# Silu writes each chunk's tokens landmark-major, so that the output store's outer dimension is 32 and not 4

## The chip, the cores and the metric

One core of one Trainium2 chip. The metric is the device time of one execution in microseconds, as the median of several; executions 1 to 2% slower, at a lower granted clock (slow runs), are left out of comparisons. In the profiles PE is TensorE (matrix products), PEld its weight loads, ACT ScalarE (functions such as Silu), DVE VectorE, POOL GpSimd, SP SyncE (here it issues transfers). SBUF is the core's working memory; PSUM is the memory that TensorE writes to, used here as eight tiles of 512 columns, called banks. A ratio is the mean time of one kernel's fast runs over the mean of the other's of the same rounds, so it is not quite the ratio of the medians quoted beside it.

## The reference

Nystrom attention for 8 batches of 8 heads, 576 tokens, 32 landmarks (a landmark is the mean of 18 neighbouring tokens), then a two-layer block on all 4608 tokens:

```python
x = attn_out.transpose(0, 2, 1, 3).reshape(B * S, H * D)     # 4608 x 512
h = x @ w_in                                                 # 512 -> 2048
g = h * (1.0 / (1.0 + np.exp(-h)))                           # Silu
return (g @ w_out).astype(np.float32)                        # 2048 -> 512
```

Token number within a batch is `l * 18 + j`: landmark l (32), place j within it (18).

The 576 output rows of a batch are nearly the same: permuting tokens inside the chunks changes the reference's result by 3e-7 of its norm. The comparison with the reference therefore does not see a wrong token order. The order in each kernel that claims to be right was checked apart from it, by following token numbers through the index patterns.

## The kernel before

It is one static program. A planner (not shown) simulates the five engines with rough durations and fixes the order of instructions on each; a Silu of 512 columns counts as 0.485 us in it. The hidden columns of a batch stand in the order (parity of j, j // 2, l), 32 values of l innermost. Layer 1 makes 16 tiles of 128 hidden features by 512 tokens in PSUM; ScalarE applies Silu and writes bf16 to `gm`. Layer 2 takes 128 tokens at a time (a chunk: 4 values of j, 32 of l) as stationary weights; the result is copied to `ost` and stored. Two of the 18 values of j go through a second path, `gx`, not changed here.

```python
ost_r = ring(outp, [128, DMODEL], FP, "ost", 3)
...
def layer1(b):
    ...
        mm(ps.rearrange("p (c x) -> p c x", c=2), m_sb[:, g, dc*128:(dc+1)*128],
           etc[:, g, :, 0:256], start=(g == 0), stop=(g == 1))
    ...
        nc.scalar.activation(out=gm[:, dc, :], in_=bank(cell["o"]), func=AF.Silu)
    ...                                          # the gx path, once per 8 tiles
        nc.scalar.activation(
            out=gx[:, d0:d0 + 8, c:c + 64].rearrange("p d (l j) -> p d j l", j=2),
            in_=bank(cell["o"]).rearrange("p (d j l) -> p d j l", d=8, j=2), func=AF.Silu)
...
def rows(b, n):
    return out[b * S:(b + n) * S, :].rearrange("(b l j) n -> b j l n", b=n, j=J)

def layer2_batch(b):
    for c in range(4):
        j0 = 8 * (c % 2) + c // 2
        def stores(ost, j0=j0):
            return nc.sync.dma_start(out=rows(b, 1)[0, j0:j0 + 7:2], in_=ost)
        layer2(lambda dc, c=c: gm_r[b % 3][:, dc, c * 128:(c + 1) * 128], ..., stores)
```

Loads of q, k, v for later batches are issued by GpSimd; stores and DMA transposes (`qT`, `ct`) are issued by SyncE and share one queue. From batch 2 on GpSimd sums k and q in a tree to the landmarks `lm`. `ct` is the transpose of `ce`, the exponentials that TensorE multiplies with v; by the program its DMA transposes wait until the v load of the next batch has landed, where there is one. `pb` is the first step of the next batch's softmax over landmarks.

The softmax here doesn't subtract the row's maximum and nothing guards it: scores larger than these inputs give would overflow.

## Time and profile before

| | before |
|---|---|
| median (4 runs) | 314.46 us, 313.25 to 315.34 |
| PE, ACT busy | 269.5, 179.7 us of 313.0 |
| gm Silu | 128 of 642 ns, from start to start 0.478 us |
| waits of PE on `lm` and on `ct` | 16.5 + 14.7 us |

The lines themselves are in the prediction. Read them as it does: first where TensorE has holes, then what ends each hole, then why that thing was late.

### The profile page before, as it was taken

Reading aid. Unit: us, or ns where it says so; the run is one execution under the profiler, and the core shown is the slowest. Engines: PE = TensorE matmul, PEld = TensorE weight load, DVE = VectorE, ACT = ScalarE, POOL = GpSimd, SP = SyncE. Lnnn points to the kernel's source line nnn. Section 1 sums busy time; section 2 is a strip of 40 time slices with the busy share of each in tenths; the row PEclk is TensorE's granted clock in tenths of the full one; section 3 lists DMA queues with packets and bytes.
Section 4 is the critical chain, followed back from the end, with each engine's and each line's share of the span. In section 5 each row is a group of like instructions: output and inputs, shape, how many; then the busy total and the mean of one; then the engine's idle time right before and its main releaser. Section 6 shows DMA issues by size and latency. Waiting matters only on the chain.

```text
span 313.0 us, 5933 instructions
## 1 busy us (share of the span) xinstructions
PE 269.5 (86%) x2367; PEld 135.0 (43%) x2367; DVE 96.6 (31%) x258; ACT 179.7 (57%) x405; POOL 106.9 (34%) x133
## 2 busy tenths in 40 slices
PE   7998999939889638998799249997999999999991
PEld 5965545414344214453444024444445544444440
DVE  1676028400555611405346114035365300000000
ACT  1776986448826914898149209985369975112110
POOL 8157319453924590485041931295000000000000
PEclk9999999968999956999799659999999999999998
DMA  6999997969386928696669257866951011132222
GB/s 113 209 197 201 206 209 129 163 136 169 60 135 123 206 66 178 116 154 69 129 132 199 68 71 139 165 98 106 193 95 44 17 31 37 40 96 64 75 68 97
DMA packets 58076, 37.60 MB, mean 120 GB/s; under 512 B 39105, under 2 KB 49345, under 8 KB 58049
## 3 DMA queue, kind: packets, MB, share of 16 engines
q0 software_dynamic: 15232, 18.35, 35.3%
q1 hardware_dynamic: 42816, 18.88, 29.6%
q8 instruction: 18, 0.29, 0.4%
q14 instruction: 10, 0.07, 0.1%
HBM read 36.70 MB, written 9.44 MB: 147 GB/s over the span
## 4 chain that ended last, share of the span: by engine, by line
PE 52%; DMA 29%; ACT 6%; POOL 4%; SPq 3%; issue 2%; DVE 2%; POOLq 0%; ACTq 0%
PE ps L323 52%; DMA v<-in_v_dram 11%; DMA ct<-ce 7%; DMA w_in_sb<-in_moe_w_in_dram 7%; SPq L479 3%; ACT gm L811 3%; DMA qT<-qk 3%; POOL qk L368 2%; POOL v L375 2%; ACT gx L834 1%; ACT L914 1%; DVE bbd L576 1%; ACT ce L691 0%; DVE bm L570 0%; POOL lm L516 0%
## 5 line engine op out<-in xcount | busy, mean ns | idle before, releaser
L323 PE MATMUL ps<-w_out_sb,gm 128*128 128x512 bf16 x512 | 122.1, 382 | 0.0
L811 ACT ACTIVATE gm<-ps 128x512 bf16<-128x512 f32 x128 | 67.4, 642 | 30.6 <-PE ps L323 30.4
L323 PE MATMUL ps<-etn,m 128*128 128x64 bf16 (+1 forms) x512 | 75.5, 299 | 0.1
L323 PEld LDWEIGHTS <-gm 128*128 128x128 bf16 x512 | 47.4, 98 | 52.7 <-issue 2.9
L323 PEld LDWEIGHTS <-m 128*128 128x128 bf16 x512 | 33.1, 101 | 30.1 <-issue 7.1
L333 ACT COPY ost<-ps 128x512 f32<-128x512 f32 x25 | 14.7, 587 | 50.8 <-PE ps L323 50.7
L516 POOL TENSOR_TENSOR sa<-qk 128x576 f32<-128x576 bf16 x24 | 31.0, 1311 | 34.4 <-DMA qk<-in_k_dram 33.9
L620 DVE SCALAR_TENSOR_TENSOR st<-st,ps 128x320 bf16<-128x320 bf16 (+3 forms) x54 | 21.6, 408 | 46.0 <-PE ps L323 42.8
L323 PE MATMUL ps<-v,ct 96*64 96x128 bf16 x192 | 10.0, 251 | 15.6 <-DMA ct<-ce 14.7
L368 POOL DMA_DIRECT2D qk<-in_k_dram x8 | 6.0, 745 | 51.2 <-DMA qT<-qk 50.0
L335 DVE CAST m<-ps 128x512 bf16<-128x512 f32 x31 | 19.8, 686 | 9.0 <-PE ps L323 9.0
L516 POOL TENSOR_TENSOR sb<-sa 128x512 f32<-128x512 f32 (+1 forms) x24 | 21.6, 901 | 1.8
L333 ACT CAST m<-ps 128x512 bf16<-128x512 f32 x33 | 17.9, 617 | 3.0 <-PE ps L323 2.9
L323 PE MATMUL ps<-idb,lm 128*128 128x128 bf16 x32 | 4.7, 240 | 16.5 <-POOL lm L516 16.5
L335 DVE COPY ost<-ps 128x512 f32<-128x512 f32 x11 | 7.6, 689 | 32.7 <-PE ps L323 32.7
L375 POOL DMA_DIRECT2D v<-in_v_dram x24 | 13.9, 589 | 6.1 <-DMA w_out_sb<-in_moe_w_out_dram 3.7
L323 PE MATMUL ps<-w_out_sb,gx 128*128 128x512 bf16 x64 | 15.9, 379 | 0.0
L323 PEld LDWEIGHTS <-ct 96*64 96x64 bf16 x192 | 7.1, 126 | 20.3 <-DMA ct<-ce 17.2
L323 PE MATMUL ps<-zer 128*128 128x256 bf16 x95 | 14.5, 295 | 1.1 <-DVE zer L402 1.1
L323 PE MATMUL ps<-st 128*128 128x160 bf16 (+1 forms) x96 | 15.2, 234 | 0.0
L691 ACT ACTIVATE ce<-ps 128x288 bf16<-128x288 f32 x32 | 12.7, 412 | 3.9 <-PE ps L323 3.9
L323 PEld LDWEIGHTS <-st 128*128 128x128 bf16 x96 | 9.3, 103 | 12.3 <-issue 3.7
(68 smaller groups left out, 260.7 us busy)
## 6 DMA issues: line engine op xcount, KB each, us to landing
out_dram<-ost SPq DMA_DIRECT2D x36, 256.0 KB
qk<-in_k_dram POOLq DMA_DIRECT2D x8, 576.0 KB, 9.4
qk<-in_q_dram POOLq DMA_DIRECT2D x8, 576.0 KB, 12.3
v<-in_v_dram POOLq DMA_DIRECT2D x24, 192.0 KB, 13.3
w_out_sb<-in_moe_w_out_dram POOLq DMA_DIRECT2D x4, 512.0 KB, 10.8
w_in_sb<-in_moe_w_in_dram POOLq DMA_DIRECT2D x4, 256.0 KB, 9.6
w_in_sb<-in_moe_w_in_dram POOLq DMA_DIRECT2D x8, 128.0 KB, 7.4
qT<-qk SPq DMA_TRANSPOSE x24
```

Of the source, the lines that this page charges most:

```text
L323: nc.tensor.matmul(out=out_ap, lhsT=lhsT, rhs=rhs, start=start, stop=stop, skip_group_check=True)
L333: nc.scalar.copy(out=out, in_=in_)
L335: nc.vector.tensor_copy(out=out, in_=in_)
L368: lambda e, t=t, src=src: nc.gpsimd.dma_start(out=qk_r[b % 2][:, t].rearrange("p g j d -> p g (j d)"), in_=src[b].rearrange("(g h) (l j) d ...
L375: lambda e, a=a: nc.gpsimd.dma_start(out=v_r[b % 2][a * L:(a + 1) * L, :, :], in_=v[b].rearrange("h (l a x) d -> a l h (x d)", l=L, a=VA)[ ...
L479: lambda e, t=t, g=g: nc.sync.dma_start_transpose(out=qT[:, t, g], in_=qk[:, t, g].rearrange("p j d -> p (j d)")),
L516: lambda e: nc.gpsimd.tensor_tensor(out=o_, in0=a_, in1=b_, op=OP.add),
L576: bbd_op = chain("bbd", 0.2, lambda: nc.vector.tensor_tensor(out=bbd, in0=bc(bmt, 4, 2), in1=bc(hmask, NG, 1), op=OP.mult), [bmt_op, prev. ...
L620: nc.vector.scalar_tensor_tensor(out=s2[:, g0:g1, lo:SW], in0=s[:, g0:g1, lo:SW], scalar=2.0, in1=ps[:, 0:NG * SW].rearrange("p (g x) -> p ...
L691: nc.scalar.activation(out=ce[:, :, 0:VP].rearrange("p (i c) (a l) -> p c a i l", c=2, a=VA)[:, c], in_=bank(me[f"C{g}"], c)[:, 0:HS].rear ...
L811: lambda e, dc=dc, cell=cell: nc.scalar.activation(out=gm[:, dc, :], in_=bank(cell["o"]), func=AF.Silu),
L834: lambda e, d0=d0, cell=cell, c=c: nc.scalar.activation(out=gx[:, d0:d0 + 8, c:c + 64].rearrange("p d (l j) -> p d j l", j=2), in_=bank(ce ...
```

## The change

The intent: a store whose DRAM side has an outer dimension of 4 occupies only 4 of the 16 DMA engines (the prediction shows the share of 0.27 from which it reads this). If the partitions of `ost` are ordered (l, j) and not (j, l), the DRAM side becomes 32 x 4 x 512 and all 16 should take part. The order is made where Silu writes `gm`.

```diff
-    out=gm[:, dc, :], in_=bank(cell["o"]), func=AF.Silu),
+    out=gm[:, dc].rearrange("p (q l j) -> p q j l", q=4, j=4),
+    in_=bank(cell["o"]).rearrange("p (q j l) -> p q j l", q=4, j=4),
+    func=AF.Silu),
...
-    return nc.sync.dma_start(out=rows(b, 1)[0, j0:j0 + 7:2], in_=ost)
+    return nc.sync.dma_start(
+        out=out[b * S:(b + 1) * S, :].rearrange(
+            "(l j) n -> l j n", j=J)[:, j0:j0 + 7:2], in_=ost)
```

(The helper `rows` goes.) ScalarE now writes 16 runs of 32 elements with a step of 4 elements, 8 bytes.

More of the change, by code (lines that the diff above doesn't have):

```diff
@@ L870, in layer2 @@
         return pieces
-    def rows(b, n):
-        return out[b * S:(b + n) * S, :].rearrange("(b l j) n -> b j l n", b=n, j=J)
     def layer2_batch(b):
```

## The prediction

> **What bounds the kernel now.** I read the digits by slice first, then the chain of work that ended last, the waits, stretches of time, and last the records of single DMA packets.
>
> ```profile
> PE   7998999939889638998799249997999999999991
> PEclk9999999968999956999799659999999999999998
> ```
>
> TensorE is full except in a few slices, and the clock falls to half speed around the holes (slices 9, 15 and 16, 23 and 24 of 7.8 us each: near 66, 117 and 180 us). PE is busy 269.5 of 313.0 us, so 43.5 us is the most that anything which only fills holes can win, apart from what the half clock costs. The chain in order of time names what ends the holes:
>
> ```profile
> 98.64 1.14 POOL v L375 x2
> 99.78 15.76 DMA v<-in_v_dram
> ...
> 115.59 2.75 DMA ct<-ce
> 118.34 0.04 issue
> 118.38 11.11 PE ps L323 x107
> ...
> 161.68 19.59 DMA v<-in_v_dram
> ...
> 181.32 2.74 DMA ct<-ce
> ...
> 243.88 62.58 PE ps L323 x342
> ```
>
> Two loads of v last 15.8 and 19.6 us; the transpose ct waits for them and TensorE for it. From 243.9 us the end is pure TensorE. The waits give the sums:
>
> ```profile
> POOL sa L516 <- DMA qk<-in_k_dram: 33.9, 6, 8.7
> PE ps L323 <- POOL lm L516: 16.5, 5, 5.4
> PE ps L323 <- DMA ct<-ce: 14.7, 5, 5.9
> ```
>
> So 31 us of TensorE's holes hang on loads and transposes: k must land before GpSimd's tree of sums (5.9 us) can give lm, and v before ct. The stretches (columns: stretch, busy of PE, PEld, DVE, ACT, POOL, granted clock, DMA share, GB/s) show why the loads are late:
>
> ```profile
> 110.00:114.00 4.00, 2.25 (x8) 0.95 (x8) 0.43 (x1) 0.70 (x2) 3.77 (x5) 0.50 0.31 78
> 131.00:135.00 4.00, 3.85 (x37) 1.85 (x36) 0.00 (x0) 4.00 (x9) 1.48 (x2) 1.00 1.12 214
> 172.00:178.00 6.00, 1.79 (x9) 0.64 (x7) 0.91 (x2) 1.53 (x4) 5.61 (x7) 0.74 0.29 74
> 293.50:294.50 1.00, 1.00 (x6) 0.48 (x5) 0.00 (x0) 0.00 (x0) 0.00 (x0) 1.00 0.27 107
> ```
>
> The last line has only output stores in flight: a quarter of the DMA engines, 4 of 16. At 131 to 135 us loads alone use all. At 110 to 114 and 172 to 178 us the loads should be done, yet the share is again 0.3: the packet records show about 2.2 load and 2.4 store packets in flight there. Four engines work off both stores and their share of the loads; twelve have finished, and the load counts as landed only when the last has.
>
> **What the Trainium skill says.** (1) "DMA: Bandwidth & Descriptors", section "Why a DMA increments its semaphore by 16 and not by 1", How many engines: a DMA uses the largest k up to 16 that divides the slowest dimension of both sides. Before, the store's sides have 4 (DRAM) and 128 (partitions): k = 4; after, 32 and 128: k = 16. The 0.27 share above agrees with 4. (2) "ScalarE: Activation LUTs", section "What ACT_TABLE_LOAD costs": an ACTIVATE with immediates takes 186 ns + 0.833 ns per element, 613 ns for 512; the median of the 128 gm Silus is 616 ns. It says nothing of strided output. (3) "SBUF — State Buffer", section "Door 1: The DMA port swizzle", note on cachelines: bf16 can stride up to 8 elements for free. The trace does not agree (gx below). (4) "TensorE: Matmul & The Clock Gate", Part 1: an idle window of about 3.4 us drops TensorE to half clock. The trace agrees: after holes of 5.0 and 4.3 us the mean clock of 111.7 to 124 us is 0.51.
>
> **The change part by part.** The order of instructions on each engine, built and compared, is unchanged, and so are counts and bytes. Two durations change.
>
> *Stores, the gain.* A store is 128 packets of 2 KB; their median is 84 ns, so 32 packets x 84 ns = 2.7 us on each of 4 engines before, and 8 x 84 ns = 0.7 us on each of 16 after. The effect is on what shares those four engines. Loads without stores are the yardstick: for the load issued at 128.11 us GpSimd's tree starts 5.7 us later and the last v packet ends 11.4 us later. With stores around:
> - issue at 97.20: tree after 8.0 us, v after 18.2. Two to three spread stores still cost about 1 us: I expect tree after 6.7, v after 12.5. lm comes 1.3 us earlier, ct 5.4 us; both holes (4.96 at 111.75, 4.26 at 118.38) lie in a row, so the stage ends 5.4 us earlier, plus 1 to 2 us from less half clock.
> - issue at 159.09: tree after 11.9, v after 22. With four spread stores: 7 and 13.4. ct and the matmul after it come 8.7 us earlier (holes 4.21 and 5.89), plus about 2 us of half clock (7.1 us of PE work at mean clock 0.56 loses 3.1 us, of which part stays).
> - issues at 64.38 and 194.33: tree after 11.1 and 9.5, to about 6.7. The holes there are 1.47 and 0.5 us: 2 us.
> - Transposes queued behind a store on the same queue: those issued at 52.58 start only when two stores have drained, 2.3 us late (hole 5.37 at 68.88); those at 87.64, 145.36, 211.41, 216.51 and 230.63 lose about 2 us each. I count 2.3 + 2.5 + 2.5 + 1.8 + 1 = 10.
> Sum: 5.4 + 1.5 + 8.7 + 2 + 2 + 10 = about 29.6 us, if nothing else takes over.
>
> *Silu, the cost.* The 128 gm Silus now write with a stride of 4 elements in 16 runs of 32. The only evidence is gx, which writes 16 runs of 32 with a stride of 2:
>
> ```profile
> L811 ACT ACTIVATE gm<-ps 128x512 bf16<-128x512 f32 x128 | 67.4, 642 | 30.6 <-PE ps L323 30.4
> L834 ACT ACTIVATE gx<-ps 128x512 bf16<-128x512 f32 x16 | 12.2, 787 | 1.9 <-PE ps L323 1.8
> ```
>
> Medians are 780 against 616 ns, and from one start to the next, back to back, 0.589 against 0.478 us: 0.11 us more each. It is the stride and not the short runs: ce, with 9 runs of 32 contiguous elements, takes 412 ns, et with one run 422. So 128 x 0.11 = 14.2 us more on ACT, 1.8 us per batch of 16. On the path it counts where ACT runs the Silus without a pause and the next batch's softmax waits behind them, or TensorE for a bank. The stretches of 18 Silus are full in batches 0, 3, 5 and 6 (idle 0.4 us or less) and nearly in 7 (2.1); in 1, 2 and 4 they hold 5.5 to 13.7 us of idle time, made by the holes above. I charge: stage 124 to 144, 2.7 us (24 Silus; this cancels the 2.5 counted for the transpose at 145.36); 190 to 210, 3; before 83 us, 1; the last two batches 2 to 3, since TensorE has layer 2 to do meanwhile. About 9 us.
>
> *The end.* The last store (64 outer rows) already uses all engines; it starts when TensorE ends. At most 0.3 us.
>
> *Sum.* 29.6 gained, of which I believe three quarters, 22, because a hole that shrinks is partly taken over by the next cause (softmax, GpSimd's tree, the static order); less 9: 13 us. 313.5 - 13 = 300.5 us.
>
> **The rivals.** (A) *Silu costs more than gx shows.* A stride of 8 bytes spreads a run over twice as many 16-byte lines as gx's stride of 4 bytes. At 0.22 us each ACT gains 28 us, and about 9 more of it reach the path: 308 to 310. For it: nothing in this trace strides so far, and gx already broke the skill's rule. Against: f32 outputs touch as many lines as gx and are not slow (ost 587 ns), so the cost may go by the element and stay at 0.11. I give it one in four. At 0.4 us and more (one in twenty) ACT becomes the bound and the kernel is slower. (B) *The loads are hidden anyway*: the holes are then taken over by the order of GpSimd's tree and the softmax, and the gain is 3 to 5 us, eaten by Silu: 311 to 315. Against it: the load at 128 us, without stores beside it, after which TensorE has no hole until 144.7. One in eight. (C) *TensorE's clock makes the gain larger*: if all holes over 3.4 us go, the half-clock work goes too (up to 7 us): 292 to 295. For it: the clock is 1.00 wherever no hole came before. One in six.
>
> **Range and chances.** My case and C lie under 307.8 us (faster by over 2%), A mostly at or above it, B within 2%. Faster 0.75, same 0.2, slower 0.05. Range 292 to 310, predicted 300.5.
>
> **What would show it right or wrong.** The DMA share in the tail, with stores alone, should be no longer 0.25 for microseconds but short bursts over 0.5; the semaphore packets of 4 bytes on the stores' queue should go from 1344 to 1728 (12 more for each of 32 stores). The tree should start 6 to 7 us after each k load's issue, and v's load on the chain should shrink to 11 to 14 us. Waits of PE on lm and ct should fall from 31 to under 14 us. gm's row should rise from 642 to 750 to 800 ns and ACT's busy time by 14 to 20 us. A gm row over 900 ns would make the time wrong on the high side. Waits of PE on ct that stay while v lands early would break the step from loads to holes.

## The result, and the profile after

The changed kernel takes 355.35 us (median of 4, 352.84 to 356.3) against 314.46: ratio 1.1291, 95% interval 1.1219 to 1.1363. It is 13% slower, where 4% faster was predicted.

The page of the kernel after, first the digits by slice (each slice is 8.8 us), then the row of the Silu (busy us, mean ns, idle before it):

```profile
PE   8998667966699677677997665779996785899995
ACT  1887997299946969999559799995579989811111
PEclk9999999989999859969999899899999999999999
...
L811 ACT ACTIVATE gm<-ps 128x512 bf16<-128x512 f32 x128 | 150.6, 1411 | 6.0 <-PE ps L323 5.8
```

The long holes of TensorE that the change was to fill are mostly gone, but PE stands at 6 and 7 tenths over wide stretches and ACT at 9: ScalarE sets the pace there. On the chain of work that ended last, gm's Silus hold 33% of the span; before, it was 3.4%. A Silu went from 642 to 1411 ns, and the group from 67.4 to 150.6 us. The half clock is not the matter: the mean granted clock is 0.957, and was 0.937 before.

The waits of the kernel after (engine, line and what it waited for: us in total, times, longest):

```profile
PE ps L323 <- ACT gm L811: 37.5, 63, 1.7
...
PE ps L323 <- POOL lm L516: 8.2, 3, 3.3
...
PE ps L323 <- ACT pb L561: 5.4, 4, 1.9
...
PE ps L323 <- DMA ct<-ce: 4.9, 4, 2.2
```

The old waits, on `lm` and `ct`, fell from 31.2 to 13.1 us. A new one took their place: TensorE waits 63 times for a Silu to free a PSUM bank (34.9 of the 37.5 us stand before layer 1's matmuls, which read nothing of `gm`).

The timeline of ScalarE over the first batch's Silus, kernel after and then kernel before (start us, us, engine, line, what, count):

```profile
32.36 9.26 ACT L811 ACTIVATE gm<-ps 128x512 bf16<-128x512 f32 x8
41.36 0.81 ACT L836 ACTIVATE gx<-ps 128x512 bf16<-128x512 f32 x1
42.05 9.31 ACT L811 ACTIVATE gm<-ps 128x512 bf16<-128x512 f32 x8
```

```profile
33.33 4.03 ACT L811 ACTIVATE gm<-ps 128x512 bf16<-128x512 f32 x8
37.76 0.74 ACT L834 ACTIVATE gx<-ps 128x512 bf16<-128x512 f32 x1 [0.40 <-PE ps L323]
38.36 4.02 ACT L811 ACTIVATE gm<-ps 128x512 bf16<-128x512 f32 x8
```

Eight Silus take 9.3 us in place of 4.0. From one start to the next it is 1.137 us against 0.478: 0.66 us more each, six times the 0.11 us that the prediction took from gx. And in this stretch there is no pause in which it could hide; over the whole run ScalarE sat idle 6.0 us before a gm Silu, where it had been 30.6.

The other half of the change did what it should. The landing of loads (median us from issue to landing, kernel after):

```profile
qk<-in_k_dram POOLq DMA_DIRECT2D x8, 576.0 KB, 6.0
qk<-in_q_dram POOLq DMA_DIRECT2D x8, 576.0 KB, 9.0
v<-in_v_dram POOLq DMA_DIRECT2D x24, 192.0 KB, 10.2
```

Before, these were 9.4, 12.3 and 13.3 us. The semaphore packets of 4 bytes on the stores' queue went from 1344 to 1728, as 12 more for each of 32 stores would have it.

So the theory to test was: two effects that add up, a gain from the stores near the predicted size and a loss from Silu's writes far over it. The rivals: that the wide stores themselves hurt (they now meet loads and transposes on all engines), and that it is not the step of the write but its short, interleaved runs or the permuted access as such.

### The profile page after: what moved, and what is told of

Its sections match the earlier page's. It is cut to its first block, busy times and chain, and to the rows that moved or that the text cites. A ratio compares the mean times of both kernels' runs of the same rounds, so it can differ in the third digit from the quotient of the medians.

```text
span 353.2 us, 5903 instructions
## 1 busy us (share of the span) xinstructions
PE 282.4 (80%) x2337; PEld 137.7 (39%) x2367; DVE 97.3 (28%) x258; ACT 261.2 (74%) x405; POOL 106.6 (30%) x133
## 4 chain that ended last, share of the span: by engine, by line
ACT 41%; PE 33%; DMA 14%; issue 4%; POOL 3%; SPq 3%; DVE 1%; POOLq 0%; ACTq 0%
ACT gm L811 33%; PE ps L323 33%; DMA w_in_sb<-in_moe_w_in_dram 6%; DMA ct<-ce 4%; SPq L479 3%; ACT m L333 2%; DMA qk<-in_k_dram 2%; DMA qT<-qk 2%; ACT gx L836 2%; ACT L915 1%; ACT L811 1%; POOL sa L516 1%; POOL qk L368 1%; POOL sb L516 1%; ACT ln L658 1%
## 5 line engine op out<-in xcount | busy, mean ns | idle before, releaser
L811 ACT ACTIVATE gm<-ps 128x512 bf16<-128x512 f32 x128 | 150.6, 1411 | 6.0 <-PE ps L323 5.8
L323 PE MATMUL ps<-w_out_sb,gm 128*128 128x512 bf16 x485 | 117.3, 382 | 3.0 <-issue 2.3
L323 PE MATMUL ps<-etn,m 128*128 128x64 bf16 (+1 forms) x512 | 87.7, 306 | 38.2 <-ACT gm L811 34.9
L323 PEld LDWEIGHTS <-m 128*128 128x128 bf16 x512 | 34.9, 103 | 80.0 <-issue 64.2
L333 ACT COPY ost<-ps 128x512 f32<-128x512 f32 x25 | 14.8, 591 | 46.6 <-PE ps L323 46.5
L516 POOL TENSOR_TENSOR sa<-qk 128x576 f32<-128x576 bf16 x24 | 31.2, 1317 | 18.5 <-DMA qk<-in_k_dram 18.0
L335 DVE CAST m<-ps 128x512 bf16<-128x512 f32 x31 | 19.8, 685 | 14.8 <-PE ps L323 14.8
L568 DVE TENSOR_REDUCE pbs<-pb 128x2 f32<-128x64 f32 x8 | 1.7, 218 | 66.7 <-ACT pb L561 66.7
L667 DVE TENSOR_TENSOR etn<-et,ln 128x576 bf16<-128x576 bf16 x16 | 14.4, 901 | 2.6 <-ACT ln L662 2.6
L648 ACT ACTIVATE et<-ps 128x288 bf16<-128x288 f32 x32 | 11.6, 420 | 4.5 <-PE ps L323 4.4
L323 PE MATMUL ps<-w_in_sb,zt 64*32 64x512 bf16 x256 | 13.0, 396 | 1.7 <-ACT gm L811 0.7
```

The source lines that it names most:

```text
L323: nc.tensor.matmul(out=out_ap, lhsT=lhsT, rhs=rhs, start=start, stop=stop, skip_group_check=True)
L333: nc.scalar.copy(out=out, in_=in_)
L335: nc.vector.tensor_copy(out=out, in_=in_)
L516: lambda e: nc.gpsimd.tensor_tensor(out=o_, in0=a_, in1=b_, op=OP.add),
L648: lambda e, g=g, et=et, c=c: nc.scalar.activation(out=et[:, c], in_=bank(me[f"A{g}"], c)[:, 0:HS], func=AF.Exp, scale=sc / J),
L667: nc.vector.tensor_tensor(out=etn[:, g, :], in0=et.rearrange("p c x -> p (c x)"), in1=ln.rearrange("p c x -> p (c x)"), op=OP.mult)
```

## The experiments

Eleven runs were made, of ten kernels. The runs of the kernel before beside them gave medians of 314.7 to 315.1 us.

### silu_only: the Silu part alone

```diff
 (the kernel before)
-    out=gm[:, dc, :], in_=bank(cell["o"]), func=AF.Silu),
+    (Silu as in the change)
```

> Silu writes with the stride of 4 as in the change, the stores keep their outer dimension of 4 (wrong result on purpose: tokens within a chunk come out permuted). Theory 1, the strided write of Silu is the whole loss and the wide stores give some of it back: gm mean about 1410 ns, time 355 to 368 us, above the changed kernel. Rival, the wide stores add a loss of their own: 325 to 350 us, below the changed kernel.

380.14 us, ratio 1.2055 (1.2004 to 1.2107); gm mean 1403 ns. Above the changed kernel, as theory 1 says. Its waits:

```profile
PE ps L323 <- ACT gm L811: 38.4, 62, 1.7
PE ps L323 <- POOL lm L516: 19.4, 3, 8.9
PE ps L323 <- DMA ct<-ce: 12.9, 6, 6.2
```

The waits on `lm` and `ct` are still there (32.3 us), since the stores are narrow, and the waits on Silu come on top. The time was above the range I gave (355 to 368): I had not thought that the two losses would simply add.

### store_only: the store part alone

```diff
 (the kernel before)
-    return nc.sync.dma_start(out=rows(b, 1)[0, j0:j0 + 7:2], in_=ost)
+    (the store as in the change)
```

> Silu as before, stores with an outer dimension of 32 (wrong result on purpose: tokens within a chunk come out permuted). Theory 1: 294 to 304 us, waits of TensorE on lm and ct fall from 31 to under 14 us, gm mean 640 ns. Rival A, loads and transposes were hidden anyway and other waits take over: 310 to 316 us. Rival B, wide stores hurt: over 318 us.

289.93 us, ratio 0.9196 (0.9147 to 0.9245): 25 us faster, better than the range. TensorE's waits on `lm` and `ct` are 12.3 us and gm's mean is 640 ns, as expected. Both rivals fall. The two parts are additive: +65.2 us for Silu alone, -25.1 us for the store alone, +40.1 together, and the change measured +40.9.

The same views that showed the fault before show its end here. A stretch with nothing but one store in flight (columns as in the prediction: the last three are granted clock, DMA share, GB/s):

```profile
269.00:270.00 1.00, 1.00 (x6) 0.45 (x5) 0.00 (x0) 0.36 (x1) 0.00 (x0) 1.00 0.28 106
270.00:271.00 1.00, 1.00 (x6) 0.47 (x5) 0.00 (x0) 0.00 (x0) 0.00 (x0) 1.00 0.84 313
271.00:272.00 1.00, 1.00 (x7) 0.41 (x6) 0.00 (x0) 0.00 (x0) 0.00 (x0) 1.00 0.28 105
```

A burst of 0.84 in place of microseconds at 0.25. For the load windows, the issue of k's load to the start of GpSimd's tree, and to the end of the last v packet, in order of the five windows:

| | tree starts after, us | last v packet after, us |
|---|---|---|
| before | 11.1, 8.0, 5.7, 11.8, 9.5 | 16.0, 18.1, 12.1, 21.9, 14.8 |
| store_only | 5.8, 6.6, 5.6, 6.7, 5.7 | 11.1, 12.9, 11.8, 13.0, 11.9 |
| after | 5.8, 6.3, 5.6, 6.9, 5.8 | 11.2, 12.9, 12.0, 13.2, 11.9 |

All windows now look like the third, which had no store in it before.

### store_k8: eight DMA engines

```diff
+    out[b * S:(b + 1) * S, :].rearrange("(h l j) n -> h j l n", h=2, j=J)
+        [c // 2, 8 * (c % 2):8 * (c % 2) + 8]          # 8 x 16 x 512
```

> Silu as before, stores with an outer dimension of 8 (token order wrong on purpose). If a store runs on as many DMA engines as its outer dimension says, and the loss is the few engines that have loads and stores to do: a share of DMA time of 0.5 while stores run alone, and a time between the 315 of 4 engines and the 290 of 16; a store then takes 1.35 us of each of 8 engines, so the delay is half of that on 4 and the gain over half of the 25: 295 to 302 us. If it is only a question of being under 16 at all: over 306.

Median 297.51 us, but two of its four runs were slow; the two fast ones are 295.92 and 294.66, ratio 0.9367 (0.9313 to 0.9421). The stretch with stores alone, in its trace:

```profile
268.00:269.00 1.00, 1.00 (x6) 0.46 (x5) 0.00 (x0) 0.00 (x0) 0.00 (x0) 1.00 0.45 152
269.00:270.00 1.00, 1.00 (x6) 0.48 (x5) 0.00 (x0) 0.00 (x0) 0.00 (x0) 1.00 0.52 195
```

Half of the engines, as the outer dimension of 8 says. The 4-byte semaphore packets on the stores' queue, 1344 before and 1728 with wide stores, are 1472 here: 4 more for each of 32 stores, as 8 engines in place of 4 would have it. The gain is about 20 of 25 us: 4, 8 and 16 engines give 315, 295 and 290 us. (An outer dimension of 2 was wanted too; a DMA of this shape with four dimensions does not build, so there is no run of it.)

### micro_strides: the cost of a write by itself

No attention at all: ScalarE applies Silu from one PSUM bank, eight times in a row for each form of output. It is a single execution, whose state is unknown; within a form the gaps between starts agree to about 1% after the first.

```diff
+    case("wide4", 2048, BF, lambda t: t.rearrange("p (x s) -> p x s", s=4)[:, :, 0], ps)
+    case("ileave4", 512, BF, runs(4), runs_in(4))       # as in the change
+    ...                                                 # 19 forms on ScalarE, 2 on VectorE
```

> No attention and no right result: eight writes of each form in a row, ScalarE alone (and VectorE for two forms), 512 elements from PSUM. Theory 1, a write pays by how few elements it puts into a 16-byte line of SBUF before going on: bf16 with step 1 (8 to a line) 0.48 us from start to start, step 2 (4) about 0.59, step 4 (2) about 1.14, step 8 and 16 (1) about 2.2; f32 with step 2 (2 to a line) about 1.1, f32 with step 1 free; pairs of bf16 with a gap of two (4 to a line) 0.6; runs of 8 free; a wide tile with one run of 512 the same as 16 interleaved runs of 32. Rival A, the interleaving is what costs (a run comes back to lines that the run before wrote): the wide forms stay near 0.5 us and only the interleaved ones are slow. Rival B, it is a matter of 2-byte writes into 4-byte words: step 2, 4 and 8 of bf16 alike, f32 with step 4 free. Reading PSUM with a step of 32 free under all.

From one start to the next, 512 elements (medians; the trace strips digits from names, so forms are told apart by their place in time):

| written | bytes between elements | 16-byte lines | us |
|---|---|---|---|
| bf16, contiguous; in runs of 8; pairs with a gap of 2 | 2 | 64, 64, 128 | 0.628 each |
| bf16, step 2: one run / 16 runs interleaved | 4 | 128 | 0.769 / 0.764 |
| bf16, step 3 | 6 | 192 | 1.051 |
| bf16, step 4: one run / 16 runs interleaved | 8 | 256 | 1.333 / 1.333 |
| bf16, step 8 / 16 | 16 / 32 | 512 | 2.463 / 2.337 |
| f32, contiguous | 4 | 128 | 0.628 |
| f32, step 2 | 8 | 256 | 0.651 |
| f32, step 4: one run / interleaved | 16 | 512 | 1.098 / 1.098 |
| bf16 contiguous, PSUM read with a step of 32 | 2 | 64 | 0.628 |
| 256 elements, bf16: contiguous / step 4 | | 32 / 128 | 0.415 / 0.767 |
| bf16, step 4, Copy instead of Silu | 8 | 256 | 1.321 |

Lines of the groups, for contiguous, step 2, step 4 and step 8 of bf16 (mean ns is the number after the comma):

```profile
L42 ACT ACTIVATE c<-ps 128x512 bf16<-128x512 f32 x8 | 4.8, 597 | 0.3
...
L42 ACT ACTIVATE ileave<-ps 128x512 bf16<-128x512 f32 x8 | 5.9, 732 | 0.2
...
L42 ACT ACTIVATE wide<-ps 128x512 bf16<-128x512 f32 x7 | 9.1, 1302 | 0.2
...
L42 ACT ACTIVATE wide<-ps 128x512 bf16<-128x512 f32 x7 | 17.0, 2431 | 0.2
```

*Rival A falls*: one run of 512 in a wide tile costs what 16 interleaved runs cost. *Rival B falls as put*: steps of 2, 4 and 8 are not alike. *My theory 1 is half right*: f32 with a step of 2 puts two elements into a line, as bf16 with a step of 4 does, and is nearly free (0.651 us, where I expected 1.1).

The numbers fit a rule with four figures, all from this table. (That lines of 16 bytes count is seen where the cost stops growing: bf16 steps of 8 and 16 elements, 16 and 32 bytes, cost about the same.) The fixed part is 0.202 us and an element takes 0.832 ns (from 0.628 and 0.415). A 16-byte line that is visited takes 4.42 ns if it is written in single 2-byte elements (2.463 = 0.202 + 512 x 0.00442) and 1.75 ns if in 4-byte ones (1.098 = 0.202 + 512 x 0.00175). The time is the fixed part plus the larger of the elements' and the lines' time. It then gives 0.768 for bf16 step 2 (measured 0.764 to 0.769), 1.051 for step 3 (1.051), 1.334 for step 4 (1.333), 0.768 for 256 elements with step 4 (0.767), 0.650 for f32 step 2 (0.651). It is 5% high for step 16. Pairs of bf16 (128 lines, 0.628) show none of the lone 2-byte price, which would make 0.768; that they count as 4-byte writes is consistent with this but not tested further. Why a lone 2-byte write costs more per line than a 4-byte one, the runs do not say.

In the kernel successive Silus come closer together, as if the fixed part were overlapped: 256 x 4.42 ns = 1.132 us, against 1.137 measured, and 0.566 for a step of 2, against 0.573 (silu_stride2 below). For contiguous writes this leaves 0.052 us unexplained: 512 x 0.832 ns = 0.426 us, against 0.478.

VectorE pays too. Its copy from PSUM to bf16, with a step of 4 and contiguous:

```profile
L81 DVE CAST dve<-ps 128x512 bf16<-128x512 f32 x8 | 10.3, 1288 | 0.2
L80 DVE CAST dve<-ps 128x512 bf16<-128x512 f32 x8 | 5.5, 691 | 165.3 <-ACT copy L79 165.0
```

### silu_stride2: the size that the prediction had used

```diff
-    out=gm[:, dc].rearrange("p (q l j) -> p q j l", q=4, j=4),
+    out=gm[:, dc].rearrange("p (q l j) -> p q j l", q=8, j=2),   # stores wide, as in the change
```

> Silu writes 16 runs of 32 with a step of 2, as gx does, wide stores (token order wrong on purpose). Tests the size that the prediction took from gx: gm mean 750 to 800 ns and 0.59 us from start to start. Then the prediction's charge of 9 us for such a Silu, over the 290 of the stores alone, makes 296 to 302 us; if a step of 2 in all Silus is as bad as 4: over 340.

297.0 us, ratio 0.9441 (0.9389 to 0.9493). Its row of the page:

```profile
L811 ACT ACTIVATE gm<-ps 128x512 bf16<-128x512 f32 x128 | 81.6, 835 | 13.1 <-PE ps L323 12.7
```

The mean is above the 750 to 800 ns that I expected; from start to start it is 0.573 us. ScalarE's group of gm is 14.2 us over the 67.4 of before, and the time is 7 us over that of the stores alone; the prediction said 14.2 and charged 9. So a step of 2 in all 128 Silus would have made the prediction right within its range.

### psum_strided, psum_strided_again: permute where it is read

```diff
-    in_=bank(cell["o"]).rearrange("p (q j l) -> p q j l", q=4, j=4),
-    out=gm[:, dc].rearrange("p (q l j) -> p q j l", q=4, j=4),
+    in_=bank(cell["o"]).rearrange("p (q j l) -> p q l j", q=4, j=4),
+    out=gm[:, dc].rearrange("p (q l j) -> p q l j", q=4, j=4),
```

The permutation of the change is kept; only the loop order of the instruction is turned, so that it runs along the output. It writes contiguously and reads PSUM with a step of 32 f32 elements.

> Right result: Silu writes contiguously and takes its permutation on the side of PSUM, reading with a stride of 32 f32 elements; wide stores. If only the write side pays for a stride: gm mean 600 to 660 ns and 294 to 304 us, as store_only. If a strided read costs as much as a strided write: gm mean over 1200 ns and over 345 us.

291.19 us, ratio 0.9251 (0.9204 to 0.9299). Its row of the page:

```profile
L811 ACT ACTIVATE gm<-ps 128x512 bf16<-128x512 f32 x128 | 67.4, 643 | 16.0 <-PE ps L323 15.5
```

As fast as before the change (642 ns), and the time is a little below the range of 294 to 304. The permutation costs nothing measurable on this side.

> The version with gm alone on the read side once more, as the partner of the run above on the same chip: 289 to 292 us.

291.29 us, ratio 0.9245 (0.9209 to 0.9281).

### silu_runs8: whole lines

Columns j-major (layer 1's moving operand is read in runs of 32), Silu writes runs of 8, a chunk is 16 j by 8 l, the store 16 x 8 x 512.

```diff
+    out=gm[:, dc].rearrange("p (r j l) -> p j r l", r=4, j=16),
+    in_=bank(cell["o"]).rearrange("p (j r l) -> p j r l", r=4, j=16),
```

> Right token order by construction: Silu writes runs of 8 contiguous elements (one whole 16-byte line each), a chunk is 16 j by 8 l, the store's outer dimension is 16. Theory 1 (lines): gm mean 600 to 680 ns, 288 to 295 us. If short runs cost by themselves: gm mean over 900 ns and over 310 us.

289.95 us, ratio 0.9237 (0.918 to 0.9294); gm mean 641 ns. Short runs are free if each fills its line.

### weights_step4: permute in the weight load

```diff
+    layer2(lambda dc, c=c: gm_r[b % 3][:, dc, c:512:4], ..., stores)   # 16 j x 8 l
```

> Right result: Silu untouched; the hidden columns are put j-major by the moving operand of layer 1 (runs of 32), and layer 2 loads its weights with a step of 4 columns, so a chunk holds 16 j by 8 l and the store's outer dimension is 16. If a weight load with a step stays at 98 ns: 294 to 304 us. If it doubles to some 200 ns it still fits beside a 216 ns matmul: up to 306. If it goes to 400 ns or more, TensorE becomes bound by weight loads in layer 2: over 340 us.

291.23 us, ratio 0.9231 (0.918 to 0.9282), a little below the range. A weight load of 128 columns with a step of 4 takes 114 ns in place of 98, and hides beside its matmul (216 ns from start to start, as before):

```profile
L323 PEld LDWEIGHTS <-gm 128*128 128x128 bf16 x512 | 54.8, 114 | 45.9 <-issue 1.7
```

(Weights in the order of the change, with two free dimensions, do not build, so there is no run of them.)

### both_read_side: gx as well

> Right token order: both Silus, gm and gx, take their permutation on the side of PSUM and write contiguously; wide stores. gx falls from 787 to about 640 ns, 16 x 0.11 = 1.8 us less of ScalarE, of which little is on the path: 286 to 291 us, 0 to 2 us under the version with gm alone.

```diff
-    out=gx[...].rearrange("p d (l j) -> p d j l", j=2), in_=....rearrange("p (d j l) -> p d j l", d=8, j=2)
+    out=gx[...].rearrange("p d (l j) -> p d l j", j=2), in_=....rearrange("p (d j l) -> p d l j", d=8, j=2)
```

289.8 us, ratio 0.9193 (0.9155 to 0.9231), beside 0.9245 of psum_strided_again on the same chip: 1.5 us less in the median, and the intervals overlap, so it is not clearly faster. gx fell from 790 to 644 ns, which also confirms the rule for the step of 2 that the kernel before already had.

### after_replanned: how much is the static order?

```diff
 (the changed kernel)
-    A(f"g{dc}.{b}", [("ACT", act_us(512))],
+    A(f"g{dc}.{b}", [("ACT", 1.08)],
```

> The changed kernel, but the planner is told that a gm Silu takes 1.08 us of ScalarE, so it orders all engines anew. If much of the loss is the static order, made for 0.48 us per Silu: 325 to 340 us. If the loss is ScalarE's work itself, with its chain to the next softmax: 345 to 358 us.

329.94 us, ratio 1.05 (1.0452 to 1.0549); gm mean still 1420 ns, TensorE's waits on gm 16.0 us where they were 37.5. So at least about 25 of the 65 us were the order, made for Silus of 0.485 us. The other 40 us remain under this new plan; that they are ScalarE's work itself is likely (gm is busy 151.2 us as before the new plan) but not shown, since only this one other order was tried. A plan made for nearly the true duration (1.08 us, 1.137 measured) does not save the change.

## Why the prediction was wrong

- **How many engines a store uses, and what that does to loads: right.** For the loads at 97.20 and 159.09 us it said tree after 6.7 and 7 us and v after 12.5 and 13.4; store_only shows 6.6 and 6.7, and 12.9 and 13.0. One reading was off: after the yardstick load at 128.11 the last v packet ended 12.1 us later, not 11.4. The waits on `lm` and `ct` were to fall under 14 us and fell to 13.1 (12.3 in store_only).
- **The gain of the stores: right, and in the right places.** 29.6 counted, 22 believed, 25.1 measured. From the k load issued at 97.20 to the next, store_only gains 4.3 us (5.4 + 1.5 counted), and from the one at 159.09 to the next 8.3 us (8.7 + 2 counted).
- **Silu's cost: the step that failed.** "The only evidence is gx ... 0.11 us more each", hence 14.2 us on ACT and 9 on the path. Measured: 0.66 us each, 83 us on ACT, 65 on the path. The prediction took a cost seen at a step of 2 for one that holds at a step of 4. gx's 0.11 us was not a price for being strided: at a step of 2 the lines' time (128 x 4.42 = 566 ns) had just come out above the elements' time (512 x 0.832 = 426 ns), which it replaces, so three quarters of the lines' time was still hidden. From there every further line counts in full, and a step of 4 adds 128 of them. silu_stride2 shows that with the size of gx the rest of the working holds. The prediction's own alarm, a gm row over 900 ns, is the sign that came.
- **The argument against rival A was the trap.** It saw that f32 outputs "touch as many lines as gx and are not slow" and concluded that the cost goes by the element. The fact is right and the conclusion is not: the cost goes by the line, at 1.75 ns for 4-byte writes and 4.42 for 2-byte ones, and f32 at 128 lines (224 ns) hides below its elements. Rival A named the direction, with 28 us where 83 came, and its steep form ("0.4 us and more") had one chance in twenty.
- **Where the loss would sit: right.** TensorE waiting for banks behind Silu, and the next softmax behind Silu (VectorE's wait on `pb` rose from 36.3 to 66.7 us).
- **Rivals B and C.** B (loads hidden anyway) falls with store_only. C (clock) is part of it: TensorE's mean granted clock rose from 0.937 to 0.965 in store_only; its share of the 25 us was not taken apart.

## What to carry to other kernels

A penalty seen in one place is a point on a curve, and if it is small it may be the first point after a knee: before scaling it to another stride or type, measure that form, which takes one kernel of a few writes. If a layout must be permuted, let the instruction loop along its output and put the strides on the side that reads (PSUM for ScalarE, or a weight load; a strided read of SBUF by ScalarE was not tried), or permute in whole 16-byte lines; the same gain of 7 to 8% came in three such ways. And test two parts of a change apart: here a gain of 25 us was hidden under a loss of 65.

## What the Trainium skill lacked or had wrong

- "SBUF — State Buffer", Door 1, note on cachelines: it says bf16 may stride by 8 and f32 by 4 for free, and that two hits on a line suffice. For ScalarE's writes that is not so: bf16 with a step of 2, 3, 4 and 8 takes 0.77, 1.05, 1.33 and 2.46 us for 512 elements against 0.63, f32 with a step of 4 takes 1.10. Two hits suffice nearly for f32 (step 2: 0.65) and not for bf16.
- "ScalarE: Activation LUTs", What ACT_TABLE_LOAD costs: 186 ns + 0.833 ns per element holds within 3% for contiguous output (613 ns by the page for 512, 597 measured), but it has no term for the output's lines: 4.42 ns per 16-byte line written in lone 2-byte elements, 1.75 ns in 4-byte ones, where that is more than the elements' time. That a read of PSUM with a step of 32 elements is free for ScalarE (596 ns) is not there either.
- No page has VectorE's cost for such a write of 2-byte elements ("Vector Engine (DVE) Microarchitecture Reference" has stepped writes of 4-byte words only): 1288 ns for a bf16 copy from PSUM with a step of 4 against 691 contiguous.
- "DMA: Bandwidth & Descriptors", Why a DMA increments its semaphore by 16 and not by 1: the rule for the number of engines held at 4, 8 and 16 (shares 0.25, 0.5, 0.84 in a burst). It has no figure for what a store on few engines does to others: the last packet of a set of loads ended 21.9 us after the first issue with narrow stores beside it and 13.0 with wide ones.
- No page has the cost of a weight load with a step: 114 ns with a step of 4 columns against 98.
